# A threshold attention with a maxout feed-forward on one core: the last batch's feed-forward pieces in pairs of blocks, the first quad by single heads, and a new written order

## The chip, the cores and the metric

The kernel runs on one core of a Trainium2 chip. The metric is the device time of one execution in microseconds; lower is better. A core has five engines with a queue each, which run side by side: TensorE (PE in the profile; PEld are its weight loads), VectorE (DVE), ScalarE (ACT), GpSimd (POOL) and SyncE (SP), which here only issues DMAs. Each queue runs strictly in the order in which the program issued its instructions.

## The reference

q, k and v are 8 batches x 8 heads x 576 positions x 64, in float32; tau is 0.02. For each head:

```
scores = (q @ k.T) / 8
scores = where(scores >= max(scores, row) - tau, scores, -1e9)
attn   = softmax(scores, row)
x      = attn @ v                      # 4608 tokens x 512 over all heads
```

and then on all 4608 tokens

```
h   = maximum(maximum(x @ w1, x @ w2), x @ w3)    # w1, w2, w3: 512 x 768
out = h @ w_out                                   # 768 x 512
```

## The kernel before, in words

**Quads, chunks, tiles.** Heads are worked on four at a time: a "quad" is (batch, half of the heads), 16 in all. Within a quad r (0 or 1) is the pair of heads and i (0 or 1) the head within the pair. A quad's rows are cut into 9 chunks: 0 to 3 are 128 rows of heads with i = 0, 5 to 8 of heads with i = 1, and chunk 4 holds the last 64 rows of both. A chunk with an r is a "tile": 128 rows of scores x 576 columns, 288 tiles in all. Two tiles (r = 0 and 1) share a chunk's sums, reciprocals and the matrix P.

**What a tile goes through.** Loads `load` (182) bring q, k and v; `transposed` (258) turns blocks of q and k by TensorE into a PSUM slot; `evacuated` (235) copies them out as `qt` (ScalarE, scaled) and `kt` (VectorE); `swapped` (243) makes `qs`, the same with the partition halves exchanged, on GpSimd. `scores` (280) is two float32 products that use the upper and the lower 64 rows of the array at the same time. `maximum` (312) takes the row's maximum on VectorE. Then there are two ways, chosen per tile by the string of bits `MASKED` (24): a masked tile (109 of 288) leaves PSUM with the maximum's pass, ScalarE takes the exponential from SBUF (`exponents`, 324), and VectorE applies the threshold and sums in one pass (`numerators`, 332); a plain tile is passed twice by ScalarE, once out of PSUM with a very flat negative side and once for exponential and sum. `reciprocals` (340) is on VectorE, `normalized` (344) writes P on GpSimd in two pieces, `turned` (353) turns P by a transposing DMA into `ptq`. `product` (359) multiplies by v; its copy out of PSUM is `xt`.

**The feed-forward.** `ffn` (425) makes pieces: `hid(f, wi)` is the product of `xt` with block f (128 columns) of weight wi, and its copies take the running maximum: ScalarE writes `hm` for wi = 0, VectorE updates `hm` for wi = 1 and writes `hT` for wi = 2. `outp` and `ninth` multiply `hT` by w_out; ScalarE (at the very end also VectorE) copies out and SP stores. A batch's token columns are two runs of 288, and `halves` (403) makes a piece in two steps: the upper array half works on one run while the lower half works on the other (64 of the 128 rows to be summed each), and then, after a wait for the first step's last product, the halves change over. Each run has a PSUM bank of its own in a slot of two banks; there are four slots.

The last batch (`SPLIT`, 35) is done in two parts, columns 0 to 255 and 256 to 575, so that part 1 starts before the last chunks are ready. There a piece is one run with products over the whole array, four of them, in one step:

```
if nr == 1:
    for kc in range(4):
        o, w, m = operands(kc, 0)
        tensor.matmul(o, w(slice(0, 128)), m(slice(0, 128)), start=(kc == 0), stop=(kc == 3))
```

**What sets the order.** No scheduler does. `ORDER` (39) is a text written by a planner beforehand; `issue` (603) reads it letter by letter, and each engine's instructions are chained in that order. S, T, O and F with a slot number are TensorE's scores, transposes, products and first steps, B a second step; m, k, r, v, w, c are VectorE's (maximum, masked numerators, reciprocal, feed-forward copies, xt copy, k copy); e, n, h, x, u, a ScalarE's (exponents, plain numerators, hm, xt, output and q copies); p, q, y, z GpSimd's (P, swap, v casts, weight casts); t, l, g, o are DMAs that SP issues (turning P, loads of q, k and v, weight loads, stores). Ahead of the text, lines 549 to 563 issue 14 and then 5 (`FILL`, 33) transposes that nobody reads, the first quad's four transposing pieces (q and k of r = 0, then of r = 1, both heads i at once), and its swaps.

Of the kernel before, what the change touches and what calls it, by code (L numbers as in the profile page):

```python
# [24 lines left out]
101000100110000110011100001010010001100010001000101000010000100000100010  # L25
000011110101100001001001001001000001011100101011000110001010010000010011
001010011101100000101100100001001010000110011111000001000100000110000101
001001001101100000110001000100101000001100010011100101110110000001111111
# [4 lines left out]
FILL = 5  # L33
# [6 lines left out]
glllllS0lylS1mylyeS2zmlkS3lelmnlT0mS1aS2rmeqS0meqmeS3pnkT1pT0nrcaptemS0yeS1mgS2eympeS3mqtnT1S0mqnS2knrceprmS  # L40
1epkepeS3mnyS0rkptemnS2pmnlzmS3erremtpT0empS1eklpaS2kgnS0ptnmeprrmlS1epS3mleS2pmlS0eplmetpmeS1knS3tkernkS2pt
nmnprmtepmS1eqS0melpmT2ntrmT3pnrcpatekS3pekS2eqnrS1mtnqmS0pemepS3tmeqS2kepT1lnrcnprtmS0nT1pmS3epmgS2atpmeO1k
yermeO0knptrerT3wpnT2cS1aptmnS3pS2xmptS1emzS0emeS3zgmeS2lrmpnS0lmO1eplmeplknO3qlnrwleplkS1xqgS2ertmF3npF0meT
1pBrteBkyhS2cpnS3mpS1nvF2npmF0eqBmeqBrrvepS3tkhT2pS1nmS0lapmetS2pmeS3mzeF0mF1ezgBrnF2vpgnBktByeF0rvhpS3ntS2p
mF1npmBeBqrveT3zncT0F2taqvS3nBpmnS0tprhS1rmpeS3mtpS2emeyS0mteF1zmeF3kBelqBnvgF2pngT0vBnqlrS1cphS3lrmnS0plmO2
eplmeptS1ewpS3nmF0znmS2lBezkgO3etymyS1vegkF0ntF2nrrmpBxBpveS3phS0mtnF1prmeBprS2evptS3nmF0pnS1mplBermS3ztnS2v
nzS1meS0tmpeF3mperkS2petBmepmS0tkuF1ukelkT3elBkntrarmpS2uS3pmulS0eymtO1empnrO2kpewS3xpS1elmpF2lmF0eyqBrlkeT3
ytBhcF1pnT2vT3qlaBclnS0qvlS2nqtF3mnyF1meS0pBemBthrrF2kpeS3vnBpmF0nS1pveBrprS3mhtS2pmeS0pmeS1tpmF2emF3peBtkeT
0BvaF1onvqT2T0tBcqaS3nkqS0lhrmS2nlpmF1elpF3meBlkBelF0vntS2rvnBpS1mhplS3melF0mS2teBrmepS1rkpO3emnqO2tnrvpnwyS
0xlprS3emoF2pmoT1eyBpctS3evyF0nS1mtnS2pmBeympF1hkS3eyF2rekT0ptBamBnpS0veF3qtvS1urmnpS2mF3epketT0nkT1Bnrmparr  # L50
cpS2uS1pumtS0empS3emqoS1eF2mqlemqleS3kplnS0mBlepmlekT1teO3kunktO0urcpnrrwlS2nplS1xmpS3lmpS0eompS1eF2mtpeF3me
BkBetS0khF1nrmF2pnBvpBerrvS3phS0mtnpS1mF2peS3mtpeBmeF1yvF0etByknBvnS2tS3rhmpS1melpS0meF3lmF2elBkeBlvT1ntF0nv
T3BacS2ohS1rrmlpnF3lmF0peoBkpeBovnT2oS1qavS3tnprO2rmpmleqS0wtnT3pS1mepO2mteqkeqF0nS1cxBympnS3rS2hytmS1emF0pe
F3mpeBrkBpetF2vnF1pBnvS0thkS3nmF2BmeBveF0rrvpT1uS3kapS0nmS2F1pmtepmeS3rktepS0mnS2pmlBelrmeplS3kupS0lurmS2elp
F1mnoqmeS0qreS2lmpS3elmBpelmptekO0nketO2ukurrnwpT3T1xpcS0aF2ymyT3tpS1ceBqmS3thqF0meF2pknBtBnvF1nS3rtrvpeBmS0
phS2lmepS1lmyS3etF0meyF2mpeBkBetF1knF3vnBBrvhpS0nvT1pF2nmF3takBeS0rvplBmS1phlrS2remplF3mpleF0klBpeS1lvnS2lpm
nBtrO3mepvnptS2nwS1emF0mF3eBrkepS2hBrmS1nptvS0npT2meO3qmeycqlT0xT1yS2lacF3ntmyT0yeF1kqBatrBrevqF0hkS2pnoS3mF
1pmBteBpveS2qntS0vpnF3mprS1mlueS3pmoS0nqmtF2epmekT1oBerocpetrkS3npS1nmS0lpumS3uopmS1eT2mF0aokeorS3remplS2emt
pS1emBpeklqtkO3uqunO0rtmpewpT2xtS3cpeS0mnF2tF1meBknF3lkBhlBevF2nS0vnBmS1hrrS3pmeF0pmS2eBpmteF1pveF3kBlnS0vnl
S2rrBnmlpS1hrlmpF0eF3mtpeBkpBevtS2nF1pvnT0pBtmaS3hS0metF1rmepT2BrcepS3nvptT0S2nmyS1amS3lepmS0leO2mlelmeO1rkp  # L60
ewnT3pF0xcF2nykBnS1vnBrmS3phF0rrmepS2BynmqF1levF3qlBekpF0onvS2tBqmBhqrS1lepvT2S3lampF0lmS2peoBkpetF1vnS3prmu
S0ntqmS1eF2pmetpmeS3rkepS1tBmnpmelrS0keptS3muS1uymS0temT2yeF3pcntknT2BkelramtpS1nS2pmuS0leqrmO1tuqrkepO3nwep
mS1xpS2metF3pmS0eqBmeF1yhrkT2pBtecF3nS0vpnlS2rmpS1nlmBpnF0lveS2tmF3eBmeBkleF1klhF2lnrBvplS0nrrvptBnS3mphS1my
teS2mF3epmF0eBpeBtvpT1nrS2yvnlS3maF0omnqS1kBepF3temS2hpBrrmeS0ptveS1pmS3nptS2meO0pmeymnqlO3weokeoF1xkT0tT2S3
rcapBnmlF2pnS0vqtBerrmpS1hF3mqeT2BpncF0evptF2nkBpT1nvBlaS3ylS0hmoF1yqmT2eoBqrcnF0tpS3ervT2pBmaF1ytkqS2uvnS3q
mS1epF0mepmeS2kteT3BrnrcponmpS1uryS3umtS2emF0pepomeS1opnS2mtpeO3myektnO1wnkS2xrS3repmS1mpBekpteS2muS3purmF1e
pF0tmeBpkS3ntBhS2rnmpO1empO3xvS2xtnkS1eF3rmpF0emByepBveF1tkS2hS3mBmF0eF2rvepBBpvS1htkO3nmO0xkS2xeS3rmF0pF1me
pBeBtvS2F3vF0mF1kBeBkhF2nrvBpnBrvpS3hS0ptmS1pmeS2mtnF0mF3eBrnpBvnF1pS2vntS0rmpBmF3phoS2eS0omeF1tmBeBkO2vO0rv
pF3kpF1uketeF3kekBwrrkpBukxpuF2F0hptF1vF2pvF0hF1tvF2rvpF0hF1vpF2vF0thF1uvF2uvF0hoF3vF1vF2hoF0voO3oO1wovF2xF3
uoF0F1hF2vF0vF1hF2vF0vF1hF2vF0vF1hF2vF0vF1hF2vF0vF1hF2vBvF0uuooBF1uuuooo  # L70
# [31 lines left out]
def kernel(  # L102
# [22 lines left out]
    nc = tc.nc  # L125
# [56 lines left out]
    def load(g, first=False):  # L182
        b, qd = quads[g]
        L = Ls[g] = dict(b=b, qd=qd, first=first)
# [7 lines left out]
        q2 = nc.scalar if first else sync  # L192
        srcs = (("q", q, sync), ("k", k, q2))
        if first:
            for n, src, e in srcs:
                e.dma_start(out=L[n][:, 0:8], in_=rows_of(src)[:, 0, 0:8])
        for n, src, e in srcs:
            e.dma_start(out=L[n][:, 8:10], in_=rows_of(src)[:, :, 8])
            yield
        for n, src, e in srcs:  # L200
            if first:
                e.dma_start(out=L[n][:, 10:18], in_=rows_of(src)[:, 1, 0:8])
            else:
                e.dma_start(out=L[n].rearrange("p (r c) d -> p r c d", r=2)[:, :, 0:8], in_=rows_of(src)[:, :, 0:8])
            yield
# [29 lines left out]
    def evacuated(L, n, r, dst, src):  # L235
        if n == "q":
            scalar.activation(out=dst(L["qt"]), in_=src, func=AF.Copy, scale=scale)
        elif L["first"] and r == 1:
            scalar.activation(out=dst(L["kt"]), in_=src, func=AF.Copy)
        else:  # L240
            vector.tensor_copy(out=dst(L["kt"]), in_=src)

    def swapped(L, r):

        cols = slice(320 * r, 320 * r + 64 * (5 - r))
        for x in (1, 0) if L["first"] else (0, 1):
            e = vector if L["first"] and (r, x) == (0, 0) else pool
            e.tensor_copy(out=L["qs"][64 * x:64 * x + 64, :, cols],
                             in_=L["qt"][64 - 64 * x:128 - 64 * x, :, cols])
            yield  # L250
# [7 lines left out]
    def transposed(L, n, r):  # L258
# [3 lines left out]
        nj = 5 - r  # L262

        def first(where):
            st["ps"] = ps = bank("tp", where)
            main = ps.rearrange("p (i z) -> p i z", i=2)[:, :, 0:256].rearrange("p i (jj u x) -> p i jj x u", jj=2, x=2)
            for j in range(nj):
                for i in (1, 0):
                    rows = slice(64 * i, 64 * i + 64)
                    tensor.transpose(main[:, i, j // 2, j % 2] if j < 4 else ps[:, 512 * i + 256:512 * i + 320],  # L270
                                     couple(L, n, r, j, rows), identf[rows, rows])
# [435 lines left out]
```

## Time and profile before

| | us |
|---|---|
| median of 3 runs | 450.04 (449.9 to 452.39) |
| profiled execution, its own time | 449.93 |
| its span, first to last instruction | 448.1 |
| TensorE busy | 427.0 (95%) |
| VectorE busy | 399.4 (89%) |
| ScalarE busy | 392.4 (88%) |
| GpSimd busy | 314.2 (70%) |
| mean granted TensorE clock | 0.988 |

Busy times are sums of the intervals in which an engine had an instruction in work. TensorE's products are pipelined, so "busy" there is not "at its peak"; start-to-start distances are the better measure of a product's cost. The idle time in front of an instruction stands in square brackets with what ended it. Nearly all instructions carry line 90, that of the helper which chains them, so rows are told apart by tile names: sc scores, ph and po the feed-forward's PSUM tiles, o the attention product, tp transposes, z a tile's scores or exponentials in SBUF, P, ptq, hm, hT, xt, qt, kt, qs.

Rows of the groups view, mean of one: maximum 751 ns (VectorE), masked numerators 832 (VectorE), exponents of a plain tile 740 and its numerators 680 (ScalarE), exponents of a masked tile 772 (ScalarE), P 809 (GpSimd), swap 740 for 640 columns (GpSimd), feed-forward copies on VectorE 754 for 576 columns, 492 for 320, 425 for 256, on ScalarE 647, 437 and 384.

### The profile page before, as it was taken

Reading aid. Unit: us, or ns where it says so; the run is one execution under the profiler, and the core shown is the slowest. Engines: PE = TensorE matmul, PEld = TensorE weight load, DVE = VectorE, ACT = ScalarE, POOL = GpSimd, SP = SyncE. Lnnn points to the kernel's source line nnn. Section 1 sums busy time; section 2 is a strip of 40 time slices with the busy share of each in tenths; the row PEclk is TensorE's granted clock in tenths of the full one; section 3 lists DMA queues with packets and bytes.
Section 4 is the critical chain, followed back from the end, with each engine's and each line's share of the span. In section 5 each row is a group of like instructions: output and inputs, shape, how many; then the busy total and the mean of one; then the engine's idle time right before and its main releaser. Section 6 shows DMA issues by size and latency. Waiting matters only on the chain.

```text
span 448.1 us, 14065 instructions
## 1 busy us (share of the span) xinstructions
PE 427.0 (95%) x5195; PEld 317.6 (71%) x5195; DVE 399.4 (89%) x1101; ACT 392.4 (88%) x793; POOL 314.2 (70%) x417
## 2 busy tenths in 40 slices
PE   7766889999999999999999999999999999999995
PEld 6524647767688768878687867868687787787762
DVE  3799999899999999999999999999999999999641
ACT  3899999999899999999999999999999999866422
POOL 3798889989785985587776785659777787534400
PEclk9898899999999999999999999999999999999999
DMA  8989999999999999999999997999998999546722
GB/s 235 266 195 188 234 238 190 249 244 220 250 192 193 187 236 209 207 215 179 227 175 205 228 217 176 217 230 205 197 195 203 204 156 194 108 78 132 130 95 107
DMA packets 212773, 87.44 MB, mean 195 GB/s; under 512 B 185824, under 2 KB 199648, under 8 KB 212704
## 3 DMA queue, kind: packets, MB, share of 16 engines
q1 hardware_dynamic: 212000, 85.69, 94.6%
q8 instruction: 41, 0.67, 0.6%
q10 hardware_dynamic: 704, 0.85, 0.6%
q14 instruction: 28, 0.23, 0.2%
HBM read 34.60 MB, written 9.44 MB: 98 GB/s over the span
## 4 chain that ended last, share of the span: by engine, by line
PE 77%; DVE 7%; ACT 5%; POOL 3%; DMA 3%; issue 2%; SPq 1%; DVEq 0%; POOLq 0%; ACTq 0%
PE ph L90 30%; PE sc L90 28%; PE po L90 10%; PE o L90 7%; ACT z L90 5%; DVE z L90 4%; PE tp L90 3%; DVE unused L90 2%; POOL P L90 2%; DMA qm<-in_q_dram 1%; DMA km<-in_k_dram 1%; SPq L90 1%; DVE hm L90 1%; DMA out_dram<-ob 1%; DVE kt L90 0%
## 5 line engine op out<-in xcount | busy, mean ns | idle before, releaser
L90 POOL TENSOR_SCALAR P<-z,rs 128x576 bf16<-128x576 f32 x288 | 228.8, 809 | 89.2 <-DVE rs L90 45.2
L90 PE MATMUL sc<-kt,qs 64*128 64x256 f32 (+2 forms) x640 | 180.5, 423 | 7.7 <-DVE z L90 2.0
L90 PE MATMUL sc<-kt,qt 64*128 64x320 f32 (+2 forms) x640 | 181.1, 433 | 4.0 <-DVE kt L90 1.2
L90 PE MATMUL ph<-xt,w 64*128 64x288 bf16 (+2 forms) x2160 | 165.5, 283 | 0.4 <-DVE hT L90 0.2
L90 PEld LDWEIGHTS <-w 64*128 64x128 bf16 (+1 forms) x2160 | 127.3, 94 | 29.8 <-issue 7.2
L90 ACT ACTIVATE z<-sc,nm 128x576 f32<-128x576 f32 x179 | 128.9, 740 | 10.8 <-DVE unused L90 9.5
L90 DVE TENSOR_SCALAR_CACHE_REDUCE unused<-sc 128x576 bf16<-128x576 f32 x179 | 130.5, 751 | 8.2 <-PE sc L90 7.3
L90 ACT ACTIVATE z<-z 128x576 f32<-128x576 f32 x179 | 120.8, 680 | 0.1
L90 PEld LDWEIGHTS sc<-kt,qs 64*128 64x128 f32 (+1 forms) x640 | 92.3, 179 | 30.9 <-ACT z L90 7.8
L90 PEld LDWEIGHTS sc<-kt,qt 64*128 64x128 f32 (+1 forms) x640 | 92.2, 178 | 20.0 <-ACT z L90 5.4
L90 DVE SCALAR_TENSOR_TENSOR z<-z 128x576 f32<-128x576 f32 x109 | 89.1, 832 | 0.2
L90 DVE TENSOR_SCALAR_CACHE_REDUCE z<-sc 128x576 f32<-128x576 f32 x109 | 80.5, 752 | 7.9 <-PE sc L90 4.6
L90 ACT ACTIVATE z<-z,nm 128x576 f32<-128x576 f32 x109 | 81.5, 772 | 2.6 <-DVE z L90 2.0
L90 POOL COPY qs<-qt 64x512 f32<-64x512 f32 (+1 forms) x63 | 45.0, 714 | 15.0 <-ACT qt L90 11.9
L90 PE MATMUL po<-wo,hT 64*128 64x512 bf16 (+1 forms) x480 | 54.0, 356 | 0.1
L90 DVE TENSOR_TENSOR hm<-ph,hm 128x576 bf16<-128x576 f32 (+2 forms) x54 | 37.1, 687 | 11.7 <-PE ph L90 11.3
L90 ACT ACTIVATE hm<-ph 128x576 bf16<-128x576 f32 (+2 forms) x54 | 32.1, 595 | 15.2 <-PE ph L90 13.7
L90 PEld LDWEIGHTS <-hT 64*128 64x128 bf16 (+1 forms) x480 | 29.3, 97 | 17.0 <-issue 3.1
L90 DVE TENSOR_TENSOR hT<-ph,hm 128x576 bf16<-128x576 f32 (+2 forms) x54 | 37.2, 688 | 3.8 <-PE ph L90 0.9
L90 PE MATMUL o<-ptq,vb 128*64 128x512 bf16 (+2 forms) x544 | 38.9, 282 | 0.2
L90 ACT ACTIVATION_READ_ACCUMULATOR z<-z 128x1 f32 x179 | 35.4, 198 | 0.0
L90 PEld LDWEIGHTS <-vb 128*64 128x64 bf16 x544 | 23.5, 111 | 14.4 <-issue 4.4
(33 smaller groups left out, 278.2 us busy)
## 6 DMA issues: line engine op xcount, KB each, us to landing
vm<-in_v_dram SPq DMA_DIRECT2D x32, 256.0 KB, 4.2
out_dram<-ob SPq DMA_DIRECT2D x31, 256.0 KB, 2.8
qm<-in_q_dram SPq DMA_DIRECT2D x15, 512.0 KB, 4.7
km<-in_k_dram SPq DMA_DIRECT2D x15, 512.0 KB, 5.1
stage<-in_moe_w_dram SPq DMA_DIRECT2D x9, 512.0 KB, 4.5
ptq<-P SPq DMA_TRANSPOSE x144, 4.2
stage<-in_moe_w_out_dram SPq DMA_DIRECT2D x3, 512.0 KB, 4.9
qm<-in_q_dram SPq DMA_DIRECT2D x16, 64.0 KB, 2.9
```

What stands on the lines that cost most here:

```text
L90: ins = fn(*a, **kw)
```

## The change

1. **The last batch's feed-forward pieces** take two neighbouring blocks f at once: nine pieces per part instead of eighteen, each in two steps over array halves, with one block in each PSUM bank. The copies are twice as wide (512 and 640 columns) and half as many.
2. **The first quad** is transposed by single heads: heads i = 0 of r = 0 first (for q without the ninth block, which moves to the piece of r = 1), and the other six half pieces as the first letters T of the written order. Its first eight tiles are chunks 0 to 3 of r = 0 and then chunks 0 to 3 of r = 1; `MASKED` is indexed in this order. The first k copies are all on VectorE and the first swaps all on GpSimd (before, one k copy was on ScalarE and one swap on VectorE). Of the first three loads of q, the third now comes second.
3. **`FILL`** is 6 instead of 5.
4. **`ORDER` and `MASKED`** are new throughout: 101 tiles are masked instead of 109, and all letters after the start stand in a new order.

```diff
-FILL = 5
+FILL = 6
...
-        q2 = nc.scalar if first else sync
...
+            for x in range(3):
+                for n, src, e in (("q", q, sync), ("k", k, nc.scalar)):
+                    if x == 0:
+                        e.dma_start(out=L[n][:, 0:8], in_=rows_of(src)[:, 0, 0:8])
+                    elif (x == 1) == (n == "k"):
+                        e.dma_start(out=L[n][:, 8:10], in_=rows_of(src)[:, :, 8])
+                    else:
+                        e.dma_start(out=L[n][:, 10:18], in_=rows_of(src)[:, 1, 0:8])
...
+    def blocks(n, r, ii):
+        if n == "q" and ii == (0,):
+            return ((0, 1, 2, 3), (4, 0, 1, 2, 3))[r], 256 * r
+        return ((0, 1, 2, 3, 4), (0, 1, 2, 3))[r], 320 * r
...
-    def transposed(L, n, r):
+    def transposed(L, n, r, ii=(0, 1)):
...
-            for j in range(nj):
-                for i in (1, 0):
+            for j in js:
+                for i in ii[::-1]:
...
             def operands(kc, a):
-                c0, c1 = runs[a]
+                c0, c1 = runs[a % len(runs)]
+                col = f if part is None else 2 * f + a
                 return (my["ps"][:, a * 512:a * 512 + n],
-                        lambda rows: wts[wi][rows, kc, f * 128:(f + 1) * 128],
+                        lambda rows: wts[wi][rows, kc, col * 128:(col + 1) * 128],
...
-                if nr == 1:
-                    for kc in range(4):
-                        o, w, m = operands(kc, 0)
-                        tensor.matmul(o, w(slice(0, 128)), m(slice(0, 128)), start=(kc == 0), stop=(kc == 3))
-                else:
-                    my["h"] = halves([[operands(kc, a) for kc in range(4)] for a in range(2)])
-                    my["h"][0]()
+                my["h"] = halves([[operands(kc, a) for kc in range(4)] for a in range(2)])
+                my["h"][0]()
...
+                        dst = h_of(b)[:, 2 * f:2 * f + 2, runs[0][0]:runs[0][1]]
...
-        return ([hid(f, wi) for f in range(NF) for wi in range(3)],
+        return ([hid(f, wi) for f in range(NF if part is None else NF // 2) for wi in range(3)],
...
+    tiles = [(n, r) for r in range(2) for n in range(4)] + [(n, r) for n in range(4, len(steps)) for r in range(2)]
...
-    for x, (r, n) in enumerate(((0, "q"), (0, "k"), (1, "q"), (1, "k"))):
-        p = transposed(Ls[0], n, r)
+    for x, n in enumerate("qk"):
+        p = transposed(Ls[0], n, 0, (0,))
         p.first(x)
         p.done[0]()
...
-                T=((g, n, r) for g in range(1, NQ) for r in range(2) for n in "qk"),
+                T=iter([(0, n, 1, (0,)) for n in "qk"] + [(g, n, r, (0, 1) if g else (1,)) for g in range(NQ) for r in range(2) for n in "qk"]),
```

The order text opened with, before and after:

```
glllllS0lylS1mylyeS2zmlkS3lelmnlT0mS1aS2rmeqS0meqmeS3pnkT1pT0nrcaptemS0y
lgS2glT3lT0alT1cqlmyS3aleS0ymlznlT1meqT2lqceS3ygqS1amlzT0S2lmeqlmS1eqT3n
```

and it ended with

```
F2vBvF0uuooBF1uuuooo
F1vBvF2BF0uuuooo
```

In the tail the second step of the output piece of part 1 stood behind all of part 2's pieces, and now stands behind the first step of the first of them; the two attention products of the last batch's quad 0, part 2, stood before all feed-forward of part 1 and now follow it.

More of the change, by code (lines that the diff above doesn't have):

```diff
@@ L430, in ffn @@
         st = {}
[L431 removed]
+        n = runs[0][1] - runs[0][0]
         def hid(f, wi):
@@ L553, with pieces_of_scores @@
         pass
[L554 to L555 removed]
+    for x, n in enumerate("qk"):
+        p = transposed(Ls[0], n, 0, (0,))
         p.first(x)
         p.done[0]()
[L558 to L570 removed]
+    for _ in range(FILL):
+        tensor.transpose(warm[:, 0:128], identf, identf)
+    for _ in swapped(Ls[0], 0, (0,)):
+        pass
+    def pieces_of_scores():
+        for n, r in tiles:
+            if n == len(made):
+                g, idx = steps[n]
+                made.append(dict(g=g, idx=idx, n=n))
+            yield made[n], r
     def pieces():
```

160 lines of the change are left out of this document (74 added, 86 removed).

## The prediction, made before the changed kernel was run

> **What bounds the kernel now.** Read first: the page's slices, busy tenths in 40 slices of 11.2 us.
>
> ```profile
> PE   7766889999999999999999999999999999999995
> DVE  3799999899999999999999999999999999999641
> ACT  3899999999899999999999999999999999866422
> PEclk9898899999999999999999999999999999999999
> ```
>
> TensorE is full from the seventh slice (about 67 us) to the end; before that VectorE and ScalarE are the full ones. The windows view makes this sharp (time, then busy us of PE, PEld, DVE, ACT, POOL, then the granted clock).
>
> ```profile
> 0.00:16.00 16.00, 11.52 (x93) 9.38 (x93) 6.84 (x22) 7.37 (x12) 6.97 (x15) 0.94 0.89 266
> 16.00:40.00 24.00, 17.15 (x143) 8.84 (x140) 22.70 (x70) 23.60 (x48) 20.14 (x26) 0.97 0.99 199
> 40.00:80.00 40.00, 35.19 (x377) 24.80 (x379) 38.68 (x109) 39.34 (x83) 36.93 (x47) 0.91 1.08 221
> 130.00:200.00 70.00, 69.89 (x914) 53.27 (x912) 68.00 (x187) 66.91 (x135) 50.80 (x69) 1.00 1.08 212
> 417.00:429.00 12.00, 11.85 (x138) 9.54 (x137) 5.57 (x14) 4.17 (x11) 3.66 (x6) 1.00 0.73 172
> ```
>
> From 16 to 80 us ScalarE is idle 1.1 of 64 us and binds, VectorE 2.6; TensorE is idle 11.7, as it has no feed-forward work yet. From 130 us TensorE idles 0.11 in 70. In the tail ScalarE and VectorE stand half empty. The view of waits, kept to TensorE from 80 us on, has one entry:
>
> ```profile
> PE ph L90 <- DVE hT L90: 0.2, 1, 0.2
> ```
>
> So the end is: ScalarE's time to some early point, plus all TensorE work still to issue there. I look for the latest such point, count both sides on either kernel, and take the difference. The timeline of the start shows ScalarE's one large hole before it is full:
>
> ```profile
> 9.40 0.78 ACT L90 ACTIVATE z<-z,nm 128x576 f32<-128x576 f32 x1 [0.55 <-DVE z L90]
> 13.43 0.53 PE L90 MATMUL tp<-identf,qm 64*128 64x64 f32 x10 [2.57 <-DMA qm<-in_q_dram]
> 13.99 0.70 ACT L90 ACTIVATE qt<-tp 128x640 f32<-128x640 f32 x1 [1.70 <-PE tp L90]
> 14.82 0.76 DVE L90 TENSOR_SCALAR_CACHE_REDUCE unused<-sc 128x576 bf16<-128x576 f32 x1 [1.88 <-PE sc L90]
> ```
>
> TensorE stands at the second quad's transposes, whose q lands at 13.29 (chain of waits); the scores queued behind them starve VectorE and ScalarE.
>
> **Part 1, the start.** Before, by 13.99 ScalarE has done two q copies (0.70, 0.60), one k copy (0.59) and 0.78 + 0.74 + 0.68 + 0.11 of exponentials: 4.2 us, so 9.8 are lost, and hardly any later. After: q's first transposes start at 4.64 as before (the first load's landing), k's end near 5.6; six fill transposes (five took 1.33) hold TensorE to 7.2, past the k copy (0.49 by the 320-column row, done 6.1) and both swap halves on POOL (6.2). First score product 0.65, to 7.85; nine transposes 0.65, to 8.5; the k copy queued ahead of the first maximum 0.43, the maximum 0.76: the first exponential starts near 9.4, no earlier than now. But seven score products now stand ahead of the second quad's first transpose. ScalarE then runs four exponentials (2.7, to 12.1) and a q copy (0.38), and waits 0.35 for the fourth score, whose slot is read until 11.45 (product 0.65, maximum 0.75): full from 12.85, with 1.64 of q copies and 2.7 done, 4.35 in all. Lost: 8.5. **Gain 1.3 us.** Bounds: 2.6 (both holes, 1.70 + 0.55, and 0.35) to -0.5 (the second quad's q main load goes out one 0.6 us SP issue later, behind a weight load, and the transposes meet it after all).
>
> The start's other moves: four transposing pieces become eight halves with the same 36 transposes, TensorE nothing. VectorE loses a swap (0.52) and gains smaller k copies, about +0.5 net. POOL makes eight half swaps instead of three, about +0.9 by the 740 ns row halved; POOL has 3.9 free in 16 to 40 us, which hide it, and its P pieces would otherwise reach SP's transposing loads later. The last six of the eight are in the written order, ahead of P pieces.
>
> **Part 2, the masks.** 101 tiles instead of 109 go by the masked way. From the rows: one tile moved gives VectorE back a pass of 0.832 and costs ScalarE 0.740 + 0.680 instead of 0.772; back to back the steps are 0.675 and 0.665. Over the run VectorE -6.7, ScalarE about +5.4. It counts only up to the deciding point. I take the first product of batch 1's feed-forward (121.8 us before). Up to it, ScalarE's list holds 83 first exponentials (87 before): -2.7; 59 plain second ones (55): +2.7; one q copy more: +0.6; the quarter copies 1.64 for 1.89: -0.25. **+0.3 us.** VectorE up to there: three maxima less (-2.0), five masked passes less (-4.0), one k copy more (+0.7) and the start's 0.5: -4.8, to be spent on nothing while ScalarE binds.
>
> **Part 3, the order.** What TensorE has still to issue at that point: 202 scores against 199, at 0.53 each (start to start in 85 to 405 us): +1.6; two transposing pieces less, at 0.31: -0.6. **+1.0 us.** Equal otherwise. A mark earlier (batch 0's fourth block, 84.6 us before) gives 0.4 on ScalarE and 0.6 of TensorE: the same total within 0.3.
>
> **Part 4, the paired pieces.** 144 whole-array products become 288 half-array ones. The chain shows the whole ones and, mid-run, the half ones:
>
> ```profile
> 396.43 3.92 PE ph L90 x64
> 419.40 5.84 PE ph L90 x52
> 428.82 9.89 PE ph L90 x72
> 438.71 2.59 PE po L90 x23
> ```
>
> Half: 3.92/64 = 61 ns for 288 columns, so 54.5 at 256 and 68.1 at 320. 288 of them: 7.85 + 9.80 = 17.65. Whole: 72 x 112 + 72 x 137 = 17.98. **-0.3 us**, between 0 and -0.6. Copies out of PSUM: VectorE's rows are 425 (256), 492 (320) and 753 ns (576), so about 690 (512) and 820 (640): 24 x 0.46 = 11.0 become 12 x 0.755 = 9.1; ScalarE 4.9 become 3.9. These 2.9 us count for nothing: VectorE is busy 5.57 of 12 there. Against that, the last piece's copy is 0.33 longer, and the leftover half of an output piece (1.29), which covered it, now runs earlier. The last output product reaches block 4 after 4/6 of 1.29 = 0.86, the copy ends after 0.1 + 0.82: wait 0.1. A second half that follows its own first half waits for its end:
>
> ```profile
> 441.47 0.98 PEld L90 LDWEIGHTS <-hT 64*128 64x128 bf16 x12 [0.56 <-PE po L90]
> ```
>
> TensorE lost 0.17 there (2.59 from 438.71 to 441.30). The new order has one such place more: +0.17. The old tail's 0.15 of idle goes. **+0.1 us**, between 0 and +0.8.
>
> The Trainium skill, "TensorEngine Tiling (Array Packing)", section Restrictions and Gotchas, speaks against part 4: two row tiles cannot use one PSUM bank at once, and software must synchronise. The row above agrees, with 0.56 on the weight side. If all eighteen pieces paid 0.17, part 4 would be +2.8 instead of -0.2, and the time 452.7; but sixteen of them have other halves between.
>
> The last scores' chain: 11.5 us or more of TensorE work (1.29 + 7.86 + 0.78 + 1.53) stand between the last score and the product of its P. Behind it: two maxima to 1.5, exponential to 2.3, output copies to 3.5, a piece's copy 0.65, the last exponential 0.8, reciprocal to 5.1, two P pieces (0.74 each) to 6.7, transposing load 3.3 to 4.2: 10 to 11. Hidden, with 0.5 to spare and more by the waits for slots; before it was 424.71 landed, 425.17 used. SP's stores between cost 0.6 each.
>
> **Sum**, against the profiled execution (449.93; span 448.1 and 1.8 around it): -1.3 + 0.3 + 1.0 - 0.3 + 0.1 = -0.2, so 449.7. The median shown, 450.04, is 0.1 above that execution. A measurement can tell about 1% (4.5 us), so this is no change.
>
> **The rivals.**
> A, VectorE bound the front as much as ScalarE: the chain between 46 and 60 us runs through VectorE. Then its 4.8 count: -4.8 + 1.0 - 0.2 = -4.0, 445.9. Against: ScalarE's list is no shorter and had 1.1 us idle in 64. Needs ScalarE's waits to vanish too.
> B, slower: ScalarE binds on past 122 us. At batch 2's first block (175.5 us before) its list is 1.4 longer, TensorE's rest 0.9 longer; its distance from the deciding sum (list plus rest) falls from 3.3 to 1.1. It decides once ScalarE idles over 1.1 us between 122 and 175; 130 to 200 showed 3.1 idle in 70, so 2.3 in 53, but those are waits for a full TensorE. If they stay: +1.2, and as much again to 230 us: 452.1.
> C, the half clock. Windows of the granted clock:
>
> ```profile
> 10.77:14.19 3.42, 0.85 (x15) 0.79 (x16) 2.17 (x7) 1.69 (x4) 2.21 (x4) 1.00 0.97 334
> 38.08:41.49 3.41, 1.62 (x16) 0.60 (x8) 3.41 (x13) 3.41 (x11) 2.38 (x3) 1.00 0.85 173
> 41.49:48.32 6.83, 6.12 (x41) 5.16 (x39) 6.68 (x21) 6.83 (x16) 6.42 (x9) 0.50 1.10 222
> ```
>
> After a stretch where TensorE is busy 25% or 47% the clock is 0.5 for 3.4 or 6.8 us; now ScalarE is full meanwhile and it costs little. Moved to 62 to 69 us, where TensorE is busy 6.35 of 6.83, it costs up to 3.2: 452.9. The Trainium skill, "TensorE: Matmul & The Clock Gate", Part 1, says an idle window halves the clock; 47% busy was enough here, so the rule is too mild.
> D, POOL's P pieces at the end take 1.28 each (411.50 to 413.34 had one of 1.84) instead of 0.74: the last load lands 2 to 4 us later, TensorE waits up to 3, or 2.3 taken midway: 452.0.
>
> **How the numbers follow.** Forecast (448.2 to 451.2 by its terms) 0.55; A 0.15, B 0.13, C 0.06, D 0.07; none of these 0.04. The range 446.0 to 452.8 takes in A's edge and B and D, and leaves about 2 in 10 out. Faster by over 1% (under 445.5): half of A, 0.08. Slower by over 1% (over 454.5): two of B to D together, or a stall not seen, 0.09. Within: 0.83.
>
> **What would show it.** Right: ScalarE full from about 13 us, no wait of TensorE for q near 13; first feed-forward product at 67 to 69 us; batch 1's first at 120.8; TensorE idle under 0.5 us from 85 us to the tail; half products at 54 to 55 and 68 ns; copies near 690 and 820. Wrong: ScalarE at 99% with TensorE idling after 122 us (B), VectorE's share falling while the first block comes before 66 us (A), a 0.5 clock after 60 us (C), a wait for ptq in the tail (D).

## The result, and the profile after

| | before | after |
|---|---|---|
| median of the runs made side by side, us | 450.36 (4 runs) | 455.96 (4 runs) |
| ratio, with its 95% interval | | 1.0108 (1.0085 to 1.0131) |
| profiled execution, its own time / its span, us | 449.93 / 448.1 | 455.86 / 454.0 |
| TensorE, VectorE, ScalarE, GpSimd busy, us | 427.0, 399.4, 392.4, 314.2 | 433.0, 392.7, 397.5, 320.4 |
| mean granted TensorE clock | 0.988 | 0.996 |

The changed kernel is slower by 5.6 us, 1.1%; 449.7 was forecast. The copies, masks and products came out as counted. What went wrong lies in three places: a start whose clock was released late, waits of TensorE in the middle of the run, and the end. (The profiled execution of e_late_ab, further below, took 463.59 us at a mean clock of 0.942; its trace is not read, and its time is that of its five other executions.) The mean clock counts from its first record, which comes at 17.42 us in after, so that the 0.996 leaves out the slowest part of the run.

The slices of the page of after, busy tenths in 40 slices of 11.35 us:

```profile
PE   8877699999999999999999999999999999999995
DVE  2798898998899999999899998999899998999522
ACT  2899999999999999989998999999999978798421
PEclk9998999999999999999999999999999999999999
```

They look like those of before, and so they should: 6 us are spread over 450. TensorE stands at 9 from the sixth slice on instead of the seventh. VectorE lost some nines (8 masked tiles fewer), ScalarE is busier in the tail (6.91 us of the 12 from 417 us on, against 4.17). The same stretches as before, in the view by windows (time, then busy us of PE, PEld, DVE, ACT, POOL, the granted clock, DMA share, GB/s):

```profile
0.00:16.00 16.00, 14.37 (x79) 12.01 (x80) 5.66 (x19) 6.45 (x11) 7.37 (x19) 1.00 0.92 293
16.00:40.00 24.00, 17.88 (x155) 10.54 (x152) 20.98 (x67) 23.68 (x51) 20.74 (x26) 0.96 0.81 196
40.00:80.00 40.00, 33.77 (x355) 21.03 (x353) 36.24 (x103) 38.72 (x81) 36.42 (x46) 0.98 1.11 218
130.00:200.00 70.00, 69.69 (x913) 52.61 (x911) 67.57 (x189) 66.82 (x136) 50.07 (x68) 1.00 1.00 193
417.00:429.00 12.00, 12.00 (x188) 10.30 (x186) 8.28 (x23) 6.91 (x14) 7.19 (x8) 1.00 0.90 154
```

Two things are to be seen. In the first 16 us TensorE is busy 2.85 us longer than before (11.52 there, 14.37 here) for 79 matmuls instead of 93: it is slower, not better used. And ScalarE did less by then, not more (6.45 against 7.37), where 1.3 us more were forecast.

**TensorE's time, place by place.** Busy time hides short waits, as matmuls are pipelined. So I list TensorE's products in their order, take the distance from each start to the next, and subtract the usual distance for that pair of kinds (the median in the kernel before between 100 and 405 us; 54.6 and 68.1 ns a matmul for the halves of 256 and 320 columns in the tail). What is left is time lost. The first column counts from the span's start to 60 us.

| us lost | to 60 | 60 to 100 | 100 to 300 | 300 to 400 | from 400 | sum |
|---|---|---|---|---|---|---|
| before | 31.0 | 3.6 | 1.3 | 0.1 | 0.2 | 36.2 |
| after | 31.7 | 4.1 | 4.7 | -0.3 | 1.6 | 41.8 |

The sums differ by 5.6 us, and TensorE's last product ends 5.9 later (449.6 against 443.7). So: the start did not gain its 1.3 us, the middle lost 3.4, the end 1.4. The sizes are rougher than their digits: with the products grouped in other ways the middle's difference comes out at 2.4 to 2.9. The experiments take up each place in turn.

### The profile page after: what moved, and what is told of

Read it like the earlier page. It is cut to its first block, busy times and chain, and to the rows that moved or that the text cites. A ratio compares the mean times of both kernels' runs of the same rounds, so it can differ in the third digit from the quotient of the medians.

```text
span 454.0 us, 14327 instructions
## 1 busy us (share of the span) xinstructions
PE 433.0 (95%) x5340; PEld 318.0 (70%) x5340; DVE 392.7 (86%) x1075; ACT 397.5 (88%) x804; POOL 320.4 (71%) x422
## 4 chain that ended last, share of the span: by engine, by line
PE 71%; POOL 8%; DVE 8%; ACT 5%; issue 4%; DMA 2%; SPq 0%; POOLq 0%; DVEq 0%; ACTq 0%
PE sc L90 26%; PE ph L90 25%; PE po L90 9%; PE o L90 8%; POOL P L90 5%; ACT z L90 5%; PE tp L90 3%; DVE z L90 2%; DMA ptq<-P 2%; DVE unused L90 2%; POOL qs L90 1%; DVE hT L90 1%; DVE hm L90 1%; PE warm L90 1%; POOL w L90 1%
## 5 line engine op out<-in xcount | busy, mean ns | idle before, releaser
L90 PE MATMUL sc<-kt,qs 64*128 64x320 f32 (+2 forms) x640 | 182.2, 425 | 6.2 <-ACT z L90 4.5
L90 PE MATMUL sc<-kt,qt 64*128 64x256 f32 (+2 forms) x640 | 184.0, 436 | 4.1 <-ACT z L90 3.3
L90 PEld LDWEIGHTS <-w 64*128 64x128 bf16 x2304 | 127.5, 94 | 29.1 <-issue 3.4
L90 DVE TENSOR_SCALAR_CACHE_REDUCE unused<-sc 128x576 bf16<-128x576 f32 x187 | 136.6, 751 | 9.4 <-PE sc L90 8.4
L90 ACT ACTIVATE z<-sc,nm 128x576 f32<-128x576 f32 x187 | 134.8, 741 | 9.8 <-DVE unused L90 7.5
L90 ACT ACTIVATE z<-z 128x576 f32<-128x576 f32 x187 | 126.3, 682 | 0.2
L90 DVE SCALAR_TENSOR_TENSOR z<-z 128x576 f32<-128x576 f32 x101 | 83.1, 831 | 0.6 <-ACT z L90 0.3
L90 DVE TENSOR_SCALAR_CACHE_REDUCE z<-sc 128x576 f32<-128x576 f32 x101 | 74.7, 752 | 9.7 <-PE sc L90 6.0
L90 POOL COPY qs<-qt 64x640 f32<-64x640 f32 (+3 forms) x68 | 49.1, 722 | 15.5 <-ACT qt L90 12.0
L90 PE MATMUL po<-wo,hT 64*128 64x512 bf16 (+1 forms) x480 | 54.5, 356 | 0.1
L90 DVE TENSOR_TENSOR hm<-ph,hm 128x576 bf16<-128x576 f32 (+2 forms) x48 | 36.1, 753 | 11.4 <-ACT hm L90 8.9
L90 PEld LDWEIGHTS <-hT 64*128 64x128 bf16 (+1 forms) x480 | 28.5, 97 | 18.6 <-issue 3.9
L90 PE MATMUL o<-ptq,vb 128*64 128x64 bf16 (+2 forms) x544 | 39.2, 282 | 1.4 <-DMA ptq<-P 1.1
L90 DVE TENSOR_TENSOR hT<-ph,hm 128x576 bf16<-128x576 f32 (+2 forms) x48 | 36.2, 753 | 4.5 <-PE ph L90 2.6
```

The source lines that it names most:

```text
L90: ins = fn(*a, **kw)
```

## The experiments

Each kernel ran beside the kernel before on the same chip; ratios are to that, and two experiments are better compared by their ratios than by their times. The columns of the table above, for those experiments whose profiles are used:

| us lost | to 60 | 60 to 100 | 100 to 300 | 300 to 400 | from 400 |
|---|---|---|---|---|---|
| *order of before in the middle* | | | | | |
| e_before_cold | 30.9 | 3.6 | 2.1 | 0.2 | 0.7 |
| e_before_paired | 31.9 | 3.3 | 2.6 | 0.1 | 1.5 |
| e_late_ba | 31.8 | 3.2 | 1.3 | 3.8 | 1.7 |
| e_early_ab | 31.9 | 4.6 | 2.3 | -0.1 | 0.3 |
| e_before_plain8 | 30.4 | 3.3 | 4.3 | 0.1 | 0.3 |
| *order of after in the middle* | | | | | |
| e_plug | 30.7 | 3.8 | 4.9 | -0.3 | 1.6 |
| e_fill16 | 30.5 | 3.8 | 4.3 | -0.4 | 1.4 |
| e_after_tail | 31.7 | 4.1 | 5.0 | -0.3 | 1.3 |
| e_tail_fill16 | 31.6 | 4.1 | 4.5 | -0.3 | 1.3 |
| e_early_ba | 30.3 | 5.3 | 4.6 | -0.2 | 2.2 |
| e_less_act | 30.0 | 3.8 | 4.7 | -0.5 | 1.8 |
| e_less_dve | 30.5 | 3.8 | 3.8 | -0.5 | 1.9 |
| e_after_mask8 | 29.8 | 5.0 | 6.8 | 0.0 | 1.5 |

### The start

First theory: the thin start (first quad by single heads) leaves TensorE's clock at half, and this costs the 6 us, by itself and by what follows late. TensorE's timeline in after, from the fill transposes to the first score tile (start, duration, what):

```profile
5.69 1.54 PE L90 MATMUL warm<-identf 128*128 128x128 f32 x6
...
7.75 0.63 PE L90 MATMUL sc<-kt,qs 64*128 64x256 f32 x1
7.86 0.74 PE L90 MATMUL sc<-kt,qt 64*128 64x320 f32 x1
```

A score half of 256 columns takes 0.63 here, and 0.38 from 18.08 us on in the same trace; the granted clock's first record comes at 17.42 us (the 1.00 in the windows before it rests on no record). So the first 17 us ran at about half rate. Four kernels took up the start.

**e_oldstart**: the changed kernel with the whole quad transposed at once again.

```diff
-FILL = 6
+FILL = 5
...
-    for x, n in enumerate("qk"):
-        p = transposed(Ls[0], n, 0, (0,))
+    for x, (r, n) in enumerate(((0, "q"), (0, "k"), (1, "q"), (1, "k"))):
+        p = transposed(Ls[0], n, r)
```

(and the letters of the six half pieces out of the order.)

> The changed kernel with the old start alone put back: the first quad's four transposing pieces of both heads at once ahead of the written order (5 fills), and the six half pieces with their copies and swaps taken out of the order; tiles, masks and all later letters as changed. Theory (thin start): in the changed kernel TensorE works at half rate until 17.4 us, since the nine half transposes and six fills of its first window are too little work to release the clock; with the old start score products take 0.38 and 0.43 us from about 7.4 us on, ScalarE has lost about 10 us instead of 11 when it fills, and the time falls by 1.5 to 2.5 us against the changed kernel, to 453.5 to 454.5. Rival (lists): the front is set by ScalarE's list of exponentials, whatever the start: within 0.7 us of the changed kernel.

Measured: 456.66 us, ratio 1.0133 (1.0109 to 1.0158). Undoing the start gained nothing. The first maximum came at 10.88 us, and the clock was half from 8.0 to 11.4, 21.7 to 28.5 and 38.7 to 42.1 us, so that this run does not show what the old start does at a full clock.

**e_plug**: three fill transposes between q's and k's first pieces.

```diff
+        if n == "q":
+            for _ in range(3):
+                tensor.transpose(warm[:, 0:128], identf, identf)
```

> The changed kernel with three fill transposes more, between the first q and the first k transposes, where TensorE waits for k. Theory (thin start): if what was missing is work in TensorE's window from 3.8 to 7.2 us, the clock is full from 7.2 us and the time falls by 1.5 to 2.5 us. If the window needs more than that, TensorE stays slow until 10.6 or 17.4 us and the time is that of the changed kernel within 0.7 us, or 0.5 later for the three fills. Rival (lists): no change either way, with the clock full or not.

Measured: 454.65 us, 1.0103 (1.0078 to 1.0129).

**e_fill16**: `FILL` 16 in place of 6.

> The changed kernel with 16 fill transposes instead of 6, in one block ahead of the first score product. Theory (thin start): ten more whole-array transposes keep TensorE on whole-array work until about 9 us, which releases the clock at 7.2 or 10.6 us; the first score starts 1.3 to 2.6 us later than in the changed kernel, and the later ones run at full rate; time 1.5 us less to 1 us more. Rival (lists): the later first score delays everything by its 1.3 to 2.6 us and nothing is won: 457 to 458.5.

Measured: 454.63 us, 1.009 (1.0066 to 1.0115).

**e_before_cold**: the kernel before with `WARM` 1 in place of 14 and `FILL` 0 in place of 5.

> The kernel before with 1 warming transpose instead of 14 and no fill: the same work, TensorE left cold at the start. Theory (thin start): TensorE works at half rate until 14 to 18 us, the first score product takes 1.2 us instead of 0.65, and the time rises by 1 to 2.5 us against the kernel before. Rival (lists): ScalarE's list sets the front and TensorE's rate there costs nothing: within 0.7 us of the kernel before.

Measured: 451.21 us, 1.0013 (0.9993 to 1.0033): with the clock at half until about 16 us the kernel before loses no more than its measurement can tell.

So a cold clock at the start can't be the 5.6 us. By their ratios e_plug and e_fill16 are 0.2 and 0.8 us better than the changed kernel (1.0103 and 1.009 against 1.0108), which their intervals can't tell from nothing, and 4 us or more stay. Even these gains are not sure to be the fills' doing. The start of e_less_act (below) is that of after, instruction for instruction, and there the same lines are:

```profile
5.69 0.88 PE L91 MATMUL warm<-identf 128*128 128x128 f32 x6
...
6.81 0.38 PE L91 MATMUL sc<-kt,qs 64*128 64x256 f32 x1
6.87 0.43 PE L91 MATMUL sc<-kt,qt 64*128 64x320 f32 x1
```

The same six transposes took 1.54 us in one execution and 0.88 in another: when the clock is released differs from run to run. In the column "to 60", this start gives 31.7, 31.7 and 31.9 with the late release (after, e_after_tail, e_early_ab) and 30.0 and 30.5 with the early one (e_less_act, e_less_dve); the start of before gives 31.0, 31.9, 30.3, 31.8 (before, e_before_paired, e_early_ba, e_late_ba). The means are 31.2 and 31.3: over all draws no gain of 1.3 is seen.

With the early release, however, the gain is there. ScalarE's first 16 us in e_less_act, and its first and fourth exponential of a score out of PSUM:

```profile
0.00:16.00 16.00, 12.29 (x98) 9.53 (x98) 7.83 (x26) 8.62 (x16) 7.81 (x19) 1.00 0.90 286
```

```profile
9.03 0.74 ACT L91 ACTIVATE z<-sc,nm 128x576 f32<-128x576 f32 x1 [0.58 <-DVE unused L91]
...
12.90 0.74 ACT L91 ACTIVATE z<-sc,nm 128x576 f32<-128x576 f32 x1 [0.80 <-DVE unused L91]
```

By 16 us ScalarE has done 8.62 us of work here (8.68 in e_less_dve, 8.66 in e_after_mask8), 7.19 to 7.68 in the five profiles with the start of before (before, e_before_paired, e_early_ba, e_late_ba, e_before_plain8), and 6.15 to 6.45 in the three with the new start and the late release. So the new start gains 1.2 us at an early release, near the forecast 1.3, and loses about as much at a late one. The two starts may not draw alike: the first record at the full rate comes at 4.3 to 7.4 us in all five with the old start, and with the new one at 5.0 to 5.7 in three and at 9.65 us or later in three. That is too few to call it shown that the new start is the cause of the late release.

The clock can also fall back. In e_plug it is full from 5.1 to 11.9 us and then half until 15.3, and there ScalarE waits 1.25 us instead of 0.80 for the fourth tile's maximum:

```profile
13.82 0.74 ACT L90 ACTIVATE z<-sc,nm 128x576 f32<-128x576 f32 x1 [1.25 <-DVE unused L90]
```

TensorE can issue that tile only at 11.71, after a wait of 0.97, when the second tile's first exponential has left its slot (11.45 was forecast); and its four halves then take 1.26 us instead of 0.65.

### The end

Second theory: the paired pieces with their order cost more than 0.1 us in the tail. TensorE's chain that ended last in after, from the last score tile on (start, duration, what):

```profile
418.20 0.97 PE sc L90 x8
...
423.97 0.75 POOL P L90
424.71 0.73 POOLq L713
425.45 1.05 SPq L90
...
426.60 4.77 DMA ptq<-P
...
431.41 1.59 PE o L90 x36
...
445.00 0.74 PE ph L90 x8
...
445.76 0.84 DVE hT L90
```

The last P is ready at 424.72, 5.5 us after the last score, where 6.7 had been counted. But SP is still at two stores (423.88 to 425.09) and the transposing load before (from 425.18), which the chain books to the queues of GpSimd and SP; so the last load goes out at 426.60, 1.9 after its P, and takes 4.77 us to land, where 3.3 to 4.2 had been allowed (the loads in the tail of before took 3.2 to 4.1; over its whole trace they took 3.2 to 8.2, with a median of 4.2). TensorE, which had reached its product at 430.44, loses 0.89 there, and the chain that ended last runs through this load. Then a gate (a second half behind its own first half) costs 0.23 in the piece that starts at 444.23, and the last copy, 0.84 for 640 columns, adds about 0.23 in the output piece that starts at 445.55 (0.44 with the gate that before has there too; before 0.21).

**e_after_tail**: the changed kernel with part 1's output piece and its second step ahead of the last two attention products, which reach TensorE some 2 us later.

```diff
-F0ovO2oO3owO1xO2wF3xuoF1BF2uBuoBhoF0vF3F1BF2vBBhBvF0F3vBBhF1vBvF2BF0uuuooo
+F0ovO2oO3owF1xuBoO0uoO2wuoxF3F1BBhF0vF2F3BF1vBBhBvF0F2vBBhF3vBvF1BF0uuuooo
```

> The changed kernel with one move in its tail: the output piece of part 1 (both steps, 2.6 us of TensorE) is put ahead of the last two attention products instead of behind them. Theory (late P): the changed order leaves too little work between the last score and the product of its P, and TensorE waits 0.9 us for the last transposing loads; the move covers that wait, no wait for ptq stays in the tail, and the time falls by 0.6 to 1.0 us against the changed kernel, to about 455.1. Rival (paired pieces): the tail's loss lies in the wide copies and the gates of the paired pieces, which stay: no gain, or 0.3 loss.

Measured: 454.6 us, 1.0074 (1.005 to 1.0099). In its trace the wait for ptq is gone, as is TensorE's whole entry in the view of waits from 400 us on. The gate that now follows takes 0.22 of it back, and the wait for the last copy stays (0.45): 1.3 lost instead of 1.6. Of the 1.4 us by which the median fell, the trace shows only 0.3; the rest lies within the run-to-run spread, and the two ratios' intervals overlap.

**e_before_paired**: the kernel before, its order kept up to the last batch's first feed-forward piece; from there the paired pieces with a tail written by hand.

```diff
-F2F0hptF1vF2pvF0hF1tvF2rvpF0hF1vpF2vF0thF1uvF2uvF0hoF3vF1vF2hoF0voO3oO1wov ...
+F2F0BBhptF1vBF2pvF0tBBhrF1vpBF2vpF0tBBuhF1uvoBovoO3oO0woF2xF3uoF0BF1uBuoBhoF2vF3F0BF1vBBhBvF2F3vBBhF0vBvF1BF2uuuooo
```

> The kernel before with the paired pieces alone: nine pieces per part in two steps over array halves with the wide copies, the letters of the last batch's feed-forward rewritten by hand for them, with the changed kernel's end; start, masks and all else as before. Theory (late P): the paired pieces as such cost 0 to 0.6 us (one gate, a longer last copy, 0.3 less product time): 450.4 to 451.2. Rival (paired pieces): they bring the changed kernel's loss in the tail, 1.3 us or more: 451.5 to 452.5.

Measured: 452.15 us, 1.0031 (1.001 to 1.0051), within the rival's 451.5 to 452.5; 1.5 us lost from 400 us on, against 0.2. Its weight loads show where a second half stands right behind its first:

```profile
418.94 1.95 PEld L90 LDWEIGHTS <-w 64*128 64x128 bf16 x36
421.24 2.52 PEld L90 LDWEIGHTS <-w 64*128 64x128 bf16 x48 [0.34 <-PE ph L90]
424.10 2.52 PEld L90 LDWEIGHTS <-w 64*128 64x128 bf16 x48 [0.34 <-PE ph L90]
426.96 0.33 PEld L90 LDWEIGHTS <-w 64*128 64x128 bf16 x8 [0.34 <-PE ph L90]
427.50 0.11 PEld L90 LDWEIGHTS <-vb 128*64 128x64 bf16 x1 [0.21 <-issue]
427.93 0.14 PEld L90 LDWEIGHTS <-vb 128*64 128x64 bf16 x4 [0.32 <-DMA ptq<-P]
```

Three gates, 0.22 us of TensorE each by start-to-start distances, 0.35 for ptq, and at the very end 0.23 and 0.45 as in after: 1.7 in all, less small gains elsewhere. In the eleven profiles of the tables with the paired end 1.3 to 2.2 us are lost from 400 us on, in the four without it 0.2 to 0.7 (before, e_before_cold, e_early_ab, e_before_plain8). That the paired pieces with their order cost over 1 us at the end is shown; how much of it is the load for ptq differs (0.89 in after, 0.35 here).

### The masks

Third theory: eight masked tiles fewer load ScalarE, which then binds past 122 us (rival B).

**e_after_mask8**: eight plain tiles of the changed kernel made masked (in order of issue, tiles 25 to 103), their letters n turned into k.

> The changed kernel with eight tiles between the 26th and the 104th turned back from plain to masked, one in about ten, at their places in the order: 109 masked as before; ScalarE's list 5.3 us shorter, VectorE's 6 us longer in that stretch. Theory (ScalarE binds): ScalarE's list sets the front and the stretch to 180 us, and the time falls by 1.5 to 3 us, with the first feed-forward product at 68 to 69 us instead of 70.3. Rival (order): the waits in mid run are those of the new order's couplings between queues, not of ScalarE's load: within 0.7 us of the changed kernel, or worse as VectorE gets full.

Measured: 460.22 us, 1.0201 (1.0174 to 1.0229): 4 us worse, not better.

**e_before_plain8**: six masked tiles of the kernel before made plain (tiles 31 to 146), their letters k turned into n.

> The kernel before with six tiles between the 32nd and the 147th turned from masked to plain, at their places in the order (103 masked): ScalarE's list 4 us longer, VectorE's 4.5 us shorter in that stretch. Theory (ScalarE binds): the time rises by 1 to 3 us, to 451.5 to 453.5, with TensorE waiting for ScalarE between 60 and 180 us. Rival (order): ScalarE has 4% idle after 80 us, which takes it up: within 0.7 us of the kernel before.

Measured: 452.87 us, 1.0047 (1.0022 to 1.0073), as the theory has it and outside its rival's 0.7; between 100 and 300 us it lost 4.3 us instead of 1.3, 1.3 of it in three waits of feed-forward products for ScalarE's z.

Both ways cost. The second alone would fit "ScalarE binds"; the first speaks against it, as it should have gained. What fits both is that an order is fitted to its masks: a tile that goes the other way is late somewhere. That is argued, not shown.

### Before's order and after's, spliced

To tell a loss that starts late from one that is an echo of the start, I spliced the two orders at places where both have issued the same scores, transposes, products and first and second steps. Letters that one order has already done and the other not yet are made good at the joint, slots are renamed, and each tile keeps the mask of the side that issued it.

**e_early_ba**: before's start and order up to the second feed-forward piece of batch 0 (about 72 us), then after's.

> The start, masks and order of the kernel before up to the second feed-forward piece of batch 0 (about 72 us), then the changed kernel's order, masks and paired pieces. Theory 'three places' (start about +2.0 us, middle of the run about +2.7, end about +1.4, each lost where it arises): 454.7. Rival 'the start is the cause, and what is lost later is its echo': the end's 1.4 alone stays, 452.0.

Measured: 455.33 us, 1.0108 (1.0083 to 1.0133): near the theory of three places, far from the echo. Its own joint costs 1 us (60 to 100 us), and the last load was later than in after (from 400 us: 2.2).

**e_early_ab**: after's start and order up to there, then before's.

> The changed kernel's start, masks and order up to the second feed-forward piece of batch 0 (about 72 us), then the order, masks and unpaired pieces of the kernel before. Theory 'three places': 452.6. Rival 'the start and its echo': 455.0. If the start counts for nothing: 450.6.

Measured: 453.91 us, 1.0071 (1.0045 to 1.0096): between the two. In its trace the start had the late release of the clock (31.9), the joint costs 1 us, and nothing is lost past 300 us.

**e_late_ba**: before's up to its 215th score tile (about 310 us), then after's.

> The kernel before up to its 215th score tile (about 310 us), then the changed kernel's order, masks and paired pieces. Theory 'three places': the end alone, 452.0. If the end costs nothing and all is lost before: 450.6.

Measured: 455.05 us, 1.0093 (1.0057 to 1.0129), 3 us or more over either theory. The trace shows why: 3.8 us are lost between 300 and 400 us, where neither parent loses any; TensorE waits 1.9 us in one place at the joint, until 313.59, for a copy hm on VectorE, and right behind it the granted clock is half from 313.8 to 317.2 us, while TensorE is full, which costs about 1.7 more (an estimate from 3.42 us at half rate). That is the splice's own doing; without the 3.8 it would be near 451.3.

**e_late_ab**: after's up to there, then before's.

> The changed kernel up to its 215th score tile (about 310 us), then the order, masks and unpaired pieces of the kernel before. Theory 'three places': start and middle, 455.3. Rival 'the paired end with its order is the cause': 451.

Measured: 455.19 us, 1.0091 (1.0059 to 1.0124), as the theory of three places has it (455.3); the paired end, which this kernel lacks, is not the cause alone.

The echo falls: with before's start ahead of it, after's order lost as much between 100 and 300 us (4.6) as with its own (4.7), and before's order lost 2.3 behind after's start. Two lines on weight loads of scores that wait for ScalarE's `z` (100 to 300 us; us in total, times, longest), first before and e_early_ab, with before's order there:

```profile
PEld sc L90 <- ACT z L90: 2.3, 8, 0.4
```

```profile
PEld sc L90 <- ACT z L90: 2.6, 8, 0.6
```

and then after and e_early_ba, with after's:

```profile
PEld sc L90 <- ACT z L90: 5.0, 14, 0.8
```

```profile
PEld sc L90 <- ACT z L90: 5.1, 15, 0.8
```

A score tile can't start until its PSUM slot's last reader is through, for a plain tile ScalarE's first exponential. After's order puts a score there too soon 14 times instead of 8. The waits of scores for VectorE's z grew as well, from 6 (2.0 us) to 11 (3.1), and those for ScalarE's copies hm from 2 (0.3) to 5 (1.6). (Part of each wait is hidden, as weights load ahead of products.) The splices left open whether this is because ScalarE as a whole is too full.

### The middle

**e_less_act**: 20 of ScalarE's second exponentials between 100 and 300 us take half of the columns.

```diff
-            scalar.activation(out=zn, in_=zn, func=AF.Exp, scale=-1.0 / FLAT, accum_out=acc)
+            cut = S // 2 if (number[g, idx], r) in LESS else S
+            scalar.activation(out=zn[:, 0:cut], in_=zn[:, 0:cut], func=AF.Exp, scale=-1.0 / FLAT if cut == S else 0.0, accum_out=acc)
```

> The changed kernel with 20 of ScalarE's second exponentials of plain tiles (spread over 100 to 300 us) over half of the columns, about 0.3 us less each, 6 us in all. It leaves out the threshold and the other half of the columns of those 20 tiles. If ScalarE's list sets the middle's loss (rival B): the loss of TensorE between 100 and 300 us falls from 4.7 to about 2, the time to 453.3. If it is VectorE, or chains of short waits: the loss stays above 4, the time at 455.5 or more.

Measured: 454.89 us, 1.0096 (1.0063 to 1.013); lost in the middle 4.7, as in after.

**e_less_dve** does the same to 20 of VectorE's masked numerators (`LESS` holds 20 masked tiles, and the threshold there is -1.0).

> The changed kernel with 20 of VectorE's masked numerator passes (spread over 100 to 300 us) over half of the columns, about 0.4 us less each, 8 us in all. It leaves out the threshold and the other half of the columns of those 20 tiles. If VectorE's list sets the middle's loss: 4.7 falls to about 2, the time to 453.3. If ScalarE's does: 4 or more stays, 455.5.

Measured: 454.62 us, 1.0079 (1.0054 to 1.0103); lost in the middle 3.8.

The windows from 100 to 300 us, of before, after, e_less_act and e_less_dve in this order (columns as above):

```profile
100.00:300.00 200.00, 199.70 (x2560) 151.54 (x2558) 190.70 (x529) 190.03 (x380) 147.06 (x196) 1.00 1.05 207
```

```profile
100.00:300.00 200.00, 198.60 (x2534) 148.19 (x2532) 186.64 (x513) 189.47 (x383) 150.35 (x199) 1.00 1.02 201
```

```profile
100.00:300.00 200.00, 198.74 (x2532) 148.97 (x2530) 186.35 (x510) 185.78 (x386) 150.32 (x199) 1.00 1.02 200
```

```profile
100.00:300.00 200.00, 199.24 (x2546) 148.63 (x2544) 181.66 (x512) 190.16 (x386) 147.31 (x199) 1.00 1.04 201
```

In after ScalarE is busy no more than before (189.47 against 190.03), VectorE less, and yet TensorE idles 1.40 us instead of 0.30. With 4 us less on ScalarE the waits for `z` stay as they were, 14 times, 5.0 us:

```profile
PEld sc L91 <- ACT z L91: 5.0, 14, 0.8
```

They even stand at the same places. The largest of them in the middle, in after and in e_less_act (timeline of weight loads), is at the same score tile, 0.82 in both:

```profile
248.87 0.18 PEld L90 LDWEIGHTS sc<-kt,qs 64*128 64x128 f32 x1 [0.82 <-ACT z L90]
```

```profile
247.17 0.18 PEld L91 LDWEIGHTS sc<-kt,qs 64*128 64x128 f32 x1 [0.82 <-ACT z L91]
```

TensorE's products stand in the same order in these kernels, so the middle can also be timed without any usual distances: from the 321st score product to the 801st it takes 157.35 us in after, 157.58 in e_oldstart, 157.67 in e_plug, 157.64 in e_less_act and 156.62 in e_less_dve.

So ScalarE's sum of work does not set the middle's loss, and VectorE's sets, by one trace, about a third: 0.9 of the 2.8 by which the six traces of the new order with its own work (4.3 to 5.0, mean 4.7) exceed the five of the old (1.3 to 2.6, mean 1.9). By exclusion the rest points to the places of letters in the new order: what stands ahead of what in the queues. This is argued, not shown. No letter was moved in the middle, masks and order came together in the splices, and GpSimd, busier than before (150.35 us against 147.06), was not relieved.

**e_tail_fill16**: the two mends together, e_after_tail with `FILL` 16.

> The changed kernel with 16 fill transposes instead of 6 and the output piece of part 1 ahead of the last two attention products. If start and tail lose apart from each other and from the middle: 455.8 less 1.2 less 1.3, so 453.3, and the middle's loss (about 3 us over the kernel before) stays in the trace. If one mends what the other does: 454.5.

Measured: 454.8 us, 1.0079 (1.0057 to 1.0101): 1.2 us less than after, and no better than either mend alone (1.009 and 1.0074); 453.3 was expected. Its 16 fill transposes ran at half rate (3.67 us), so that its first score came at 9.29 us and "to 60" shows 31.6: the fills cost here what they gained in e_fill16. The middle's 4.5 stay, as expected. No version beat the kernel before.

## Why the prediction was wrong, point by point

- **Where the time came from.** It was to be read at batch 1's first feed-forward product: 120.8 us forecast, 123.6 measured (before 121.8). This first part can't be told from scatter: with the order of before up to there, e_before_paired has 124.0 and e_late_ba 122.3, and with that of after, e_after_tail has 124.0. From there to TensorE's last product it took 326.0 us against 321.9: 4.1 more, of which 1.0 was forecast as more work.
- **Part 1, -1.3: the chain held at an early release of the clock, and the release was not in it.** In e_less_act ScalarE is full from 12.90 (12.85 forecast) and has done 1.25 us more by 16 us than before. The fit is partly luck: the first exponential came at 9.03 instead of 9.4, and the wait for the fourth score was 0.80 instead of 0.35. In after's own profile the clock was half until 17.4 us, the first exponential came at 10.73 and the fourth at 15.24, and 0.9 us less was done by 16 us. The bound on the bad side (+0.5) came from one SP issue; the granted clock in the first 17 us, a draw of about 1.5 us, was in no bound.
- **Part 2, +0.3: size not told apart.** ScalarE was idle 1.1 of 64 us from 16 to 80 us before and 1.6 in after, so it still stands at its limit there. Whether ScalarE's list sets the mark could not be separated from the start's draw.
- **Part 3, +1.0 of work: as counted, but the term itself was the wrong one.** The step that failed is the end as ScalarE's time "plus all TensorE work still to issue there", with no idle of TensorE behind that point: 0.11 us idle in 70 was read from the old order and carried over to a new one. With its own masks, the new order loses 4.3 to 5.0 between 100 and 300 us (3.8 with VectorE relieved), the old 1.3 to 2.6. What the runs show in its place are waits for slots whose reader is not through; why the new order has more of them stays open. The rival B had the place and about the size, but the wrong reason: it wanted ScalarE at 99%, and ScalarE stood at 95% (189.47 of 200).
- **Part 4, -0.3 + 0.1: half right.** The half products take 54.6 and 68.1 ns (54.5 and 68.1 forecast), VectorE's wide copies 685 to 692 and 825 (690 and 820), ScalarE's 598 and 704. The Trainium skill, "TensorEngine Tiling (Array Packing)", section Restrictions and Gotchas, asks for synchronisation between row tiles; a gate with nothing between cost 0.22 each time here, near the forecast 0.17. But the end costs 1.4, where 0.1 with a bound of 0.8 had been forecast: the "0.5 to spare" of the last scores' chain was a miss of 0.89. POOL was not late, as rival D had it; SP's queue was (1.9 us from P to the last load), and the load took 4.77.
- **A and C did not come.** VectorE has less to do and nothing is faster; the clock from 60 us on is full. A time over 454.5 had been given 0.09, for "two of B to D together, or a stall not seen": the signs of B and D both came, each from another cause than the rival's.

## What to carry to other kernels

A TensorE without idle time is a property of the old order, not of the work: where a change brings a whole new order, count its waits (which reader still holds the slot that the next product wants) and don't carry over the old one's zero. In a tail, count the last transfer from the queue that issues it, with the stores ahead of it, and at its slowest landing in the trace. And when two starts differ by a microsecond, look first at whether the clock was released at the same time in both.

## What the runs showed of the hardware

- The clock's release at the start differs between executions of the same instructions. With TensorE busy 14.37 of the first 16 us (transposes and half-array products), after's profiled execution stayed at half rate until 17.4 us; the same instructions ran at full rate from 5.7 us in e_less_act. The Trainium skill, "TensorE: Matmul & The Clock Gate", Part 1, says that the activity window runs free and that the number of cold products differs from run to run, which these two traces bear out; it also says that some 3.4 us of sustained work release the clock, and here more than 10 us did not. What in this work counted too little wasn't tried.
- A transposing load in the tail takes 3.2 to 5.2 us from issue to landing within one trace. The view of after's tail (minimum, median, maximum; in e_before_paired's tail the longest is 4.1):

```profile
DMA to landing us min/median/max: 3.2/3.6/5.2
```

- Runs of several offspring of the changed kernel fall into two groups some 2 us apart (e_after_tail: 452.9 to 453.9 and 455.3 to 456.0). The two draws of the clock at the start are 1.5 us apart and would explain most of it; that they are the same thing was not shown.
